# Attention into an activated two-layer product on one core: key blocks in runs of 4, 4, 3, 3, values and first weights in other pieces, and a new order table

## The chip, the cores and the metric

The kernel runs on one core of one Trainium2 chip. A core has TensorE (PE; its weight loads are listed as PEld), VectorE (DVE), ScalarE (ACT), GpSimd (POOL), SyncE (SP, used here to issue transfers) and 16 DMA engines, which the queues of SP and GpSimd share. TensorE's results stand in PSUM, everything else on the chip in SBUF. The metric is the device time of one execution in microseconds.

## The reference

```python
def _attn_ref(q, k, v):                       # 8 x 12 x 448 x 64, float32
    scores = matmul(q, k.T) / sqrt(64) - log(448)
    return matmul(1 / (1 + exp(-scores)), v)
# x: the 12 heads side by side: 3584 tokens x 768
h = x @ w_in                                  # 768 x 2048
g = h * (1 / (1 + exp(-beta * h)))            # beta: one number per hidden column
return g @ w_out                              # 2048 x 768, float32 out
```

The weight is a sigmoid, not a softmax, so no row sum is needed.

## The kernel before

**Layout.** A batch has 448 tokens, cut into 14 blocks of 32. A "group" g is four heads of one batch, three groups per batch and 24 in all; each is loaded as q and k with 32 partitions per head (`load_one`), cast to 16 bits by the transfer. VectorE turns q (`transpose(g, 0)`, step R{g}.0) and k (R{g}.1) with 32x32 transposes, so that the 64 values of a head stand on 32 partitions, in pairs. Keys are used in three full tiles of 128 and a last one of 64 (`JF` = 3, `KL` = 64). Which key of a batch stands in which row of a tile is free as long as k and v agree: before, row group i (32 rows) of the three full tiles holds blocks 3i, 3i+1, 3i+2, and the last tile holds blocks 12 and 13. So v is loaded with four transfers of three blocks and two of one block (`move_v`), and k is turned in two pieces of 384 and 64 words. `double_v_last` (step E) copies the last tile's v to the other 64 partitions.

**Stages.** "Visits" V{g}.{jt} make scores for key tile jt of the four heads (TensorE), then weights by a sigmoid (ScalarE, 128x896). A{g} multiplies the weights with v and VectorE casts the result to xT. In batch 0 the groups 0 to 2 are done in halves of the queries instead (h for scores, y and z for the two parts of the product with v). Then the first dense layer: for all but the first parts of batch 0 with Strassen-Winograd products, steps I{b}.{d}.{p} for P1 to P7, column block d; weight sums S1 to S4 are made once (steps S{i}.{part}, VectorE), token sums are steps X. For batch 0, the first eight column blocks of 128 (dc 0 to 3 and 8 to 11) are done as direct products instead: `dense1`, step f{dc} for the first 224 tokens and D0.{dc} for the other 224. Sigmoid and product with the hidden value follow: on ScalarE and VectorE for the direct blocks, P2 and P3, and on ScalarE and GpSimd in G and B. The second layer is direct for the first two token tiles (O{t}.{half}.{part}) and Winograd after that (U{t}.{p}.{part}, token sums H, weight sums T). Stores go out on SP's queue.

**Order.** Every instruction stands in the order of a table written out by hand or by a planner outside of the kernel: `OPENING`, then `STEPS`. `follow` walks it, and each engine gets its own instructions of the steps in that order. A step such as `w3` puts the transfer of a part of w_in on GpSimd's queue at that place, `v0` the values of batch 0, `Q3` q and k of group 3, `o1.0` a quarter of w_out, `K1` the values of batch 1. `i4` runs four idle units: matmuls on zeros of 512 columns each. GpSimd issues each of its transfers only when the transfer eight places earlier on its queue has landed, since eight semaphores go round. `RAW_HOMES` and `OUT_HOMES` give the buffer for each load and each output in turn. PSUM holds score tiles of two banks each (three at first, two after step p0) and single banks; `bank()` takes the one used longest ago.

**Columns.** Where the next attention step is A or y, `dense` runs each matmul as two halves of 64 output partitions.

**First data.** The first half of q and all of k of group 0 come in 32 bits on SP's queue into the still unused `gt`, are cast by VectorE and ScalarE (`key_cast`) and turned in pieces (`key_turn`). Beta is third on SP's queue.

Of the kernel before, what the change touches and what calls it, by code (L numbers as in the profile page):

```python
# [13 lines left out]
def kernel(  # L14
# [10 lines left out]
    nc = tc.nc  # L25
# [124 lines left out]
    def move_v(queue, to, b: int, h0: int, h1: int):  # L150
        rows = v[b, h0:h1].rearrange("h (p c) d -> p h (c d)", c=NB)
        for i in range(HQ):
            queue.dma_start(
                out=to[i * BLK : (i + 1) * BLK, h0:h1, 0:JF].rearrange("p h j d -> p h (j d)"),
                in_=rows[:, :, JF * i * D : JF * (i + 1) * D],
            )
        rows = v[b, h0:h1].rearrange("h (p c) d -> p h c d", c=NB)
        for c in range(NF, NB):
            lo = (c - NF) * BLK
            queue.dma_start(out=to[lo : lo + BLK, h0:h1, JF], in_=rows[:, :, c])  # L160

    def load_v(b: int, h0: int = 0):
        vs[b] = vp.tile([P, H, JF + 1, D], FP16, tag="v16", name="v16")
        move_v(nc.gpsimd, vs[b], b, h0, H)

    def double_v_last(b: int, h0: int = 0):
        nc.vector.tensor_copy(out=vs[b][KL:P, h0:, JF], in_=vs[b][0:KL, h0:, JF])  # L167

    WCH = 8
    WOUT = 2  # L170

    def load_w_in(c: int):
        n = DFF // WCH
        nc.gpsimd.dma_start(  # L174
            out=w_in16[:, :, c * n : (c + 1) * n],
            in_=moe_w_in[:, c * n : (c + 1) * n].rearrange("(c p) f -> p c f", p=P),
        )
# [34 lines left out]
    def transpose(g: int, r: int, c0: int = 0, c1: int = NB):  # L212
        raw = raws[g][:, r]
        if r == 0:
# [9 lines left out]
        frm = raw.rearrange("p c d -> p (c d)").bitcast(FP32).rearrange("p (c f) -> p c f", c=NB)  # L224
        nc.vector.transpose(
            out=to[:, 0 : JF * P].rearrange("p (j i q) -> p i j q", j=JF, i=HQ),
            in_=frm[:, 0:NF].rearrange("p (i j) f -> p i j f", j=JF),
        )
        nc.vector.transpose(
            out=to[:, JF * P :], in_=frm[:, NF:].rearrange("p c f -> p (c f)")  # L230
        )
# [231 lines left out]
    def wino1(b: int, d: int, p: str):  # L463
# [26 lines left out]
        if p == "P1":  # L490
            nc.scalar.copy(out=osbs[b, d, "a"][:, 0], in_=m)
# [132 lines left out]
    IN_HALVES = 22  # L624

    def store(t: int, lo: int, hi: int):
        osb = osbs[t]
        c, end = t * P, (t + 1) * P
        while c < end:
# [8 lines left out]
            cut = (lo + hi) // 2 if t == IN_HALVES else hi  # L638
# [12 lines left out]
    def share_anew():  # L651
# [9 lines left out]
        "f": lambda dc: dense1(0, dc, 0, QH),  # L661
        "r": lambda g, half: transpose(g, 0, half * NH, (half + 1) * NH),
# [4 lines left out]
        "v": load_v,  # L667
# [27 lines left out]
    def follow(steps):  # L695
# [15 lines left out]
        I0.2.4 E1 I0.3.5 B0.2.0 A3 G0.2 V4.0 I0.3.3 I0.3.7 o1.1 Q7 R5.1 G0.3 O0.0.0 O1.0.0  # L711
        R5.0 V4.2 O0.0.1 Q8 B0.2.1 O0.0.2 I0.3.4 O1.0.1 O1.0.2 V4.3 O1.0.3 B0.3.0 A4 V5.1
        O1.0.4 O1.0.5 O0.0.3 O1.0.6 S1.0 O0.0.4 S3.0 B0.3.1 O1.1.0 R6.1 V5.2 O0.1.0 O0.0.5
        O0.0.6 O1.1.1 R6.0 O0.1.1 S2.0 V5.0 O0.1.2 S4.0 O1.1.2 O1.0.7 O0.1.3 O0.0.7 O1.1.3
        V6.2 O0.1.4 O1.1.4 K2 X1.0 T3.0 T2.0 A5 V6.1 O1.1.5 O1.1.6 R7.0 O1.1.7 O0.1.5 O0.1.6
        I1.3.1 X1.1 R7.1 R8.0 X1.2 V6.0 I1.3.6 I1.3.5 I1.3.2 Q9 R8.1 O0.1.7 V6.3 E2 I1.3.3
        A6 V7.1 T3.1 I1.2.1 I1.3.7 X1.3 G1.3 I1.2.6 I1.2.5 Q11 V7.0 I1.3.4 T2.1 I1.2.2
        B1.3.1 I1.0.1 I1.2.3 B1.3.0 I1.2.7 G1.2 V7.2 I1.0.6 I1.0.5 I1.2.4 R9.0 I1.0.7 I1.0.2
        B1.2.0 B1.2.1 I1.0.3 I1.1.1 G1.0 I1.0.4 B1.0.0 I1.1.6 B1.0.1 Q10 I1.1.5 I1.1.2
        I1.1.7 I1.1.3 V8.0 I1.1.4 B1.1.0 T1.1 A7 B1.1.1 V8.1 R9.1 U2.1.0 U2.1.1 H2.0 H2.1  # L720
        I2.0.1 T4.0 Q12 V8.2 U2.2.0 T1.0 U2.2.1 U2.6.0 K3 H2.2 U2.6.1 H2.3 V8.3 G1.1 T4.1
        U2.5.0 X2.0 U2.5.1 A8 V9.1 K4 U2.3.0 H4.0 U2.3.1 H4.1 U4.1.0 R11.0 U2.7.0 V9.2
        U4.1.1 R11.1 U2.7.1 U4.6.0 U4.6.1 Q13 V9.0 E3 U2.4.0 U2.4.1 H4.2 R10.0 H4.3 R10.1
        U4.5.0 U4.2.0 U4.5.1 U4.2.1 X2.1 X2.3 U4.7.0 U4.7.1 U4.3.0 X2.2 V10.0 U4.3.1 I2.0.6
        U4.4.0 U4.4.1 A9 V10.3 I2.0.5 R12.1 I2.0.2 I2.1.1 I2.1.6 I2.0.3 V10.1 I2.1.2 I2.0.7
        I2.1.5 G2.0 I2.1.7 I2.0.4 I2.1.3 V10.2 I2.1.4 Q15 G2.1 R13.1 I2.2.1 B2.0.0 I2.2.6
        A10 B2.1.0 B2.0.1 V11.0 I2.2.2 B2.1.1 I2.2.5 R13.0 I2.2.7 I2.3.1 I2.2.3 V11.1 I2.2.4
        B2.2.0 I2.3.6 B2.2.1 I2.3.5 G2.2 I2.3.2 I2.3.7 U6.1.0 I2.3.3 V11.2 I2.3.4 R12.0 X3.0
        U6.1.1 B2.3.1 A11 B2.3.0 V12.2 X3.1 H6.0 U6.2.0 H6.1 Q14 U6.2.1 X3.3 I3.0.1 V12.0
        H6.2 I3.0.6 E4 X3.2 G2.3 I3.0.5 U6.6.0 R15.1 U6.6.1 H6.3 V12.1 U6.5.0 U6.5.1 I3.0.2  # L730
        I3.0.7 V12.3 I3.0.3 U6.3.0 R14.0 I3.0.4 U6.7.0 U6.7.1 U6.3.1 A12 B3.0.1 R15.0 B3.0.0
# [12 lines left out]
        I4.3.7 I4.3.3 V17.1 I4.3.4 U12.2.1 U12.5.0 G4.3 B4.3.0 X5.0 U12.5.1 A17 X5.1 V18.1
        B4.3.1 X5.3 I5.0.1 Q23 U12.3.0 U12.7.0 I5.0.6 V18.0 H14.0 U12.7.1 U12.3.1 I5.0.2
# [39 lines left out]
    with tc.manual_schedule():  # L785
# [42 lines left out]
        def key_cast(copy, j: int):  # L828
            copy(out=whole[1][:, :, j], in_=whole[0][:, :, j])
# [50 lines left out]
```

## Time and profile before

| what | value |
|---|---|
| time, median of 3 runs | 367.81 us (366.64 to 368.26) |
| the profiled execution: time / span | 367.32 us / 365.6 us |
| instructions on PE, DVE, ACT, POOL | 3819, 528, 414, 204 |
| moved by DMA | 34.79 MB in 42892 packets, mean 95 GB/s |
| granted TensorE clock | 1.00 |

The span is from the first to the last instruction; the time has 1.7 us around it. Rows of the chain that ended last give start, length, and what the time was spent on. Rows in order of time give start, length, engine, line, operation, out<-in, shape and count; in brackets stands how long the engine was idle before and what ended that. Rows of windows give the busy time (and count) of PE, PEld, DVE, ACT and POOL, then the granted clock, the DMA engines' share, and GB/s. DMA shares above 1 mean that packets overlap.

### The profile page before, as it was taken

What the parts mean: (1) busy time and instruction counts of PE and PEld (TensorE: products, weight loads), DVE (VectorE), ACT (ScalarE), POOL (GpSimd) and SP (SyncE); (2) the same over time, 40 slices, a digit from 0 to 9 for tenths busy, and PEclk for the clock granted to TensorE, in tenths of its full rate; (3) what the DMA queues carried; (4) which work ended last, traced back from release to release, by engine and by line L of the source; (5) the groups of instructions that cost most, each with busy time, mean ns of one, the idle gap of its engine ahead of it and who ended that gap; (6) DMA issues with size and microseconds to landing.
All of it is one profiled execution on the core that took longest, in us unless ns stands there. A gap on an engine that the chain in (4) does not pass through costs nothing.

```text
span 365.6 us, 9439 instructions
## 1 busy us (share of the span) xinstructions
PE 358.9 (98%) x3819; PEld 241.0 (66%) x3819; DVE 279.6 (76%) x528; ACT 250.5 (69%) x414; POOL 168.9 (46%) x204
## 2 busy tenths in 40 slices
PE   7989999999999999999999999999999999999996
PEld 2568654587456785676766676657855688878564
DVE  5439969999977789776787876778768568888755
ACT  5988897799744898775778768766895776537110
POOL 6834486158840376323785444152541026528400
PEclk9999999999999999999999999999999999999999
DMA  8999999930995213153977810694001210110235
GB/s 165 168 198 201 195 204 206 209 61 10 159 180 131 31 23 52 34 105 68 105 123 98 145 45 2 138 127 90 0 4 29 60 45 2 43 29 19 48 81 174
DMA packets 42892, 34.79 MB, mean 95 GB/s; under 512 B 21968, under 2 KB 39520, under 8 KB 42848
## 3 DMA queue, kind: packets, MB, share of 16 engines
q0 software_dynamic: 36688, 22.47, 44.8%
q1 hardware_dynamic: 6160, 11.71, 12.6%
q8 instruction: 30, 0.49, 0.6%
q14 instruction: 14, 0.11, 0.1%
HBM read 45.62 MB, written 11.01 MB: 155 GB/s over the span
## 4 chain that ended last, share of the span: by engine, by line
PE 88%; DMA 6%; POOL 3%; DVE 1%; issue 1%; ACT 0%; POOLq 0%; DVEq 0%; ACTq 0%
PE m_ps L192 70%; PE sco L239 10%; PE av_ps L321 8%; DMA raw<-in_q_dram 3%; DMA raw<-in_k_dram 2%; POOL gt L540 2%; DMA v<-in_v_dram 1%; POOL raw L133 0%; DVE sum L406 0%; POOL gt L530 0%; DVE qT L217 0%; ACT osb L459 0%; DVE v L167 0%; POOL w_in L174 0%; ACT sg L459 0%
## 5 line engine op out<-in xcount | busy, mean ns | idle before, releaser
L251 ACT ACTIVATE attnT<-sco 128x896 f16<-128x896 f32 (+1 forms) x163 | 139.0, 908 | 41.0 <-PE sco L239 40.3
L406 DVE TENSOR_TENSOR osb<-m_ps,osb 128x448 f32<-128x448 f32 (+2 forms) x217 | 127.3, 597 | 49.0 <-PE m_ps L192 35.6
L540 POOL TENSOR_TENSOR gt<-osb,sg 128x448 f16<-128x448 f32 x60 | 68.4, 1157 | 65.3 <-ACT sg L459 65.3
L192 PEld LDWEIGHTS <-w_in 128*128 128x128 f16 (+1 forms) x942 | 76.9, 101 | 14.0 <-issue 7.5
L192 PE MATMUL m_ps<-xT,w_in 128*128 128x224 f16 (+1 forms) x708 | 73.1, 259 | 1.3 <-DMA w_in<-in_moe_w_in_dram 1.2
L530 POOL TENSOR_TENSOR gt<-osb,sg 128x448 f16<-128x448 f32 x30 | 34.5, 1154 | 81.3 <-ACT sg L459 54.1
L459 ACT ACTIVATE sg<-osb,beta_sb 128x448 f32<-128x448 f32 (+1 forms) x120 | 62.5, 576 | 9.3 <-DVE osb L406 8.5
L192 PEld LDWEIGHTS <-sum 128*128 128x128 f16 (+1 forms) x488 | 40.3, 101 | 26.9 <-issue 4.6
L192 PEld LDWEIGHTS <-w_S 128*128 128x128 f16 (+1 forms) x630 | 51.0, 101 | 9.4 <-issue 5.5
L192 PEld LDWEIGHTS <-gt 128*128 128x128 f16 (+1 forms) x434 | 36.2, 100 | 26.3 <-issue 8.5
L192 PE MATMUL m_ps<-w_out,gt 128*128 128x384 f16 (+2 forms) x314 | 53.1, 323 | 0.0
L239 PE MATMUL sco<-qT,kT 32*128 32x448 f16 (+3 forms) x864 | 51.6, 339 | 0.8 <-DVE kT L832 0.5
L192 PE MATMUL m_ps<-xs,w_S 128*128 128x224 f16 (+1 forms) x408 | 42.3, 259 | 0.0
L192 PE MATMUL m_ps<-w_out,sum 128*128 128x384 f16 (+1 forms) x256 | 41.2, 327 | 0.0
L192 PE MATMUL m_ps<-w_T,sum 128*128 128x384 f16 (+1 forms) x232 | 40.4, 326 | 0.2 <-DVE sum L406 0.2
L335 DVE CAST xT<-av_ps 128x448 f16<-128x448 f32 (+1 forms) x54 | 28.2, 564 | 13.2 <-PE av_ps L321 12.9
L321 PE MATMUL av_ps<-attnT,v 128*64 128x448 f16 (+3 forms) x400 | 38.2, 343 | 0.0
L459 ACT ACTIVATE osb<-m_ps,beta_sb 128x224 f32<-128x224 f32 x56 | 22.1, 450 | 16.0 <-PE m_ps L192 10.5
L321 PEld LDWEIGHTS <-v 128*64 128x64 f16 (+1 forms) x432 | 21.2, 108 | 16.8 <-issue 9.5
L239 PEld LDWEIGHTS <-kT 32*128 32x128 f16 (+1 forms) x864 | 13.5, 96 | 22.5 <-issue 19.5
L192 PE MATMUL m_ps<-xT,w_S 128*128 128x224 f16 (+1 forms) x222 | 22.3, 260 | 0.0
L192 PE MATMUL m_ps<-xs,w_in 128*128 128x224 f16 (+1 forms) x234 | 22.1, 260 | 0.0
(55 smaller groups left out, 285.9 us busy)
## 6 DMA issues: line engine op xcount, KB each, us to landing
out_dram<-osb SPq DMA_DIRECT2D x96, 96.0 KB, 1.9
raw<-in_k_dram POOLq DMA_DIRECT2D x23, 224.0 KB, 5.2
raw<-in_q_dram POOLq DMA_DIRECT2D x21, 224.0 KB, 3.7
v<-in_v_dram POOLq DMA_DIRECT2D x32, 144.0 KB, 5.9
w_in<-in_moe_w_in_dram POOLq DMA_DIRECT2D x8, 384.0 KB, 11.3
w_out<-in_moe_w_out_dram POOLq DMA_DIRECT2D x4, 768.0 KB, 11.9
v<-in_v_dram POOLq DMA_DIRECT2D x16, 48.0 KB, 6.0
out_dram<-osb SPq DMA_DIRECT2D x4, 192.0 KB, 1.9
```

The lines of the kernel that those rows point to most:

```text
L192: nc.tensor.matmul(to[c : c + step], hidden[:, c : c + step], weights, **({} if step == P else {"tile_position": (0, c)}), **flags,)
L239: nc.tensor.matmul(sco[base : base + nk, hh, u0 : u0 + n], kT[g][lo : lo + BLK, jt * P : jt * P + nk, e], qT[g][lo : lo + BLK, c0 : c0 + n ...
L251: nc.scalar.activation(out=at[:, :, 0:n], in_=sco[:, :, 0:n], func=AF.Sigmoid, bias=NEG_LOG_S, scale=MSCALE,)
L321: nc.tensor.matmul(av[hh * D : (hh + 1) * D, 0:n], vs[b][base : base + nk, 2 * (s % NPAIR) + hh, jt], at[base : base + nk, hh, 0:n], start ...
L335: nc.vector.tensor_copy(out=xTs[b][:, s % NPAIR, c0 : c0 + n], in_=av[:, 0:n])
L406: nc.vector.tensor_tensor(out=out, in0=in0, in1=in1, op=op)
L459: nc.scalar.activation(out=out, in_=in_, func=AF.Sigmoid, bias=0.0, scale=beta_sb[:, dc : dc + 1])
L530: nc.gpsimd.tensor_tensor(out=gt[:, 2 * d : 2 * d + 2, off : off + QH], in0=ob[:, 0], in1=sg, op=ALU.mult)
L540: nc.gpsimd.tensor_tensor(out=gt[:, dc, off : off + S].rearrange("p (h n) -> p h n", h=2), in0=oa[:, :, j], in1=sg, op=ALU.mult,)
```

## The change

- Keys: the row groups hold runs of 4, 4, 3 and 3 blocks (blocks 0 to 3, 4 to 7, 8 to 10, 11 to 13). v comes with four transfers per batch, in rows of 1024 and 768 bytes as read, instead of six; k is turned in pieces of 256 and 192 words.
- The values of batch 0 come in two parts, four heads (v0.0) and eight heads (v0.1), of four transfers each, and E for them in two steps (e0.0, e0.1).
- w_in comes in five parts instead of eight: two eighths (w0, w1), then three quarters (w2, w3, w4).
- Beta is the first transfer on GpSimd's queue, not the third on SP's; the memset of `dummy` goes from GpSimd to VectorE. In the opening k of group 1 is issued ahead of the first half of its q.
- Blocks 10, 9, 0 and 2 of batch 0 are done at full width (step F: 448 tokens), not as f and D0.
- P1 of batch 0 is copied out of PSUM by VectorE instead of ScalarE.
- Output tile 25 is stored in two halves, as tile 22 was.
- The table and both lists of buffers are new. OPENING and STEPS have 13 idle units instead of 19; ahead of them stand 8 and one of 384 columns instead of 9 and one of 256.

```diff
-        rows = v[b, h0:h1].rearrange("h (p c) d -> p h (c d)", c=NB)
-        for i in range(HQ):
-            queue.dma_start(
-                out=to[i * BLK : (i + 1) * BLK, h0:h1, 0:JF].rearrange("p h j d -> p h (j d)"),
-                in_=rows[:, :, JF * i * D : JF * (i + 1) * D],
-            )
-        for c in range(NF, NB):
-            lo = (c - NF) * BLK
-            queue.dma_start(out=to[lo : lo + BLK, h0:h1, JF], in_=rows[:, :, c])
+    RUNS = ((0, JF + 1), (JF + 1, JF + 1), (2 * JF + 2, JF), (3 * JF + 2, JF))
+    GROUP0 = (0, HQ), (HQ, H)
+        rows = v[b, h0:h1].rearrange("h (p c) d -> p h (c d)", c=NB)
+        for i, (c, n) in enumerate(RUNS):
+            nc.gpsimd.dma_start(
+                out=vs[b][i * BLK : (i + 1) * BLK, h0:h1, 0:n].rearrange("p h j d -> p h (j d)"),
+                in_=rows[:, :, c * D : (c + n) * D],
+            )
...
+    def turn_keys(to, raw, i: int, j0: int, j1: int):
+        to = to.rearrange("p (a b) -> p a b", b=2 * BLK)[:, i::2]
+        n = JF + 1 - i
+        c = 2 * i * (JF + 1) * D // PAIR
+        frm = raw[:, c : c + 2 * n * D // PAIR].rearrange("p (i j q) -> p i j q", i=2, j=n)
+        nc.vector.transpose(
+            out=to[:, j0:j1].rearrange("p j (i q) -> p i j q", i=2), in_=frm[:, :, j0:j1]
+        )
...
-    WCH = 8
+    W_IN = (0, DFF // 8, DFF // 4, DFF // 2, 3 * DFF // 4, DFF)
...
-            nc.scalar.copy(out=osbs[b, d, "a"][:, 0], in_=m)
+            copy = nc.scalar.copy if b else nc.vector.tensor_copy
+            copy(out=osbs[b, d, "a"][:, 0], in_=m)
...
-    IN_HALVES = 22
+    IN_HALVES = (22, 25)
...
+        "F": lambda dc: dense1(0, dc),
...
-        idle_units(9)
-        idle_units(1, 256)
+        idle_units(8)
+        idle_units(1, 384)
```

The new order up to I0.2.3, the step on which the prediction's sum hangs:

```diff
     OPENING
+        k1 h0.0.0 l1.0.0 h0.0.1 i1 R1.1 k2 r1.0 i1 i1 i1 i1 l1.0.1 h1.0.0 l2.0.0 l0.0.1 i1
+        R2.1 i1 v0.0 r0.1 r2.0 h1.0.1 i1 i1 e0.0 r1.1 i1 i1 v0.1 h2.0.0 y0.0 w0 z0.0 h2.0.1
+        y1.0 e0.1 w1 z1.0 h1.1.0 b0 w2 y2.0 z2.0 l2.0.1 h0.1.0 i1 f1 h0.1.1 w3 i1 p0 Q3 f3
+        r2.1 y0.1 h1.1.1 z0.1 I0.3.1 I0.2.1 h2.1.0 y1.1 z1.1 X0.0 w4 I0.2.2 I0.3.2 h2.1.1
     STEPS
+        R3.0 f8 f11 y2.1 Q4 z2.1 R3.1 K1 X0.1 o0.0 Q5 X0.3 o1.0 F10 D0.1 D0.8 o0.1 D0.11
+        S1.1 V3.2 S3.1 R4.0 F9 o1.1 D0.3 V3.1 S2.1 R4.1 Q6 F0 F2 X0.2 V3.0 I0.2.6 I0.2.5
+        V3.3 S4.1 I0.2.7 I0.3.6 V4.1 I0.2.3 E1 I0.2.4 A3 V4.0 I0.3.5
...
```

The old order of the same stretch:

```diff
     OPENING
-        l1.0.0 h0.0.0 k1 b0 l2.0.0 i4 r1.0 k2 R1.1 h0.0.1 v0 R2.1 l0.0.1 i4 l1.0.1 h1.0.1 i4
-        w0 w1 w2 r2.0 h1.0.0 i2 i2 h2.0.1 E0 w3 i3 h2.0.0 r0.1 y0.0 z0.0 h0.1.0 r1.1 y1.0
-        l2.0.1 z1.0 h0.1.1 y2.0 z2.0 w4 p0 h1.1.0 Q3 w5 f1 f0 f3 r2.1 I0.2.1 h1.1.1 y0.1
-        z0.1 I0.3.1 h2.1.0 y1.1
     STEPS
-        R3.0 z1.1 I0.3.2 I0.2.2 w6 h2.1.1 w7 Q4 X0.0 f9 f2 y2.1 z2.1 X0.1 X0.3 f8 D0.10 D0.9
-        R3.1 o0.0 K1 D0.1 D0.0 D0.2 Q5 S1.1 S2.1 V3.1 D0.11 D0.8 D0.3 S3.1 V3.2 I0.2.6
-        I0.2.5 o1.0 V3.3 X0.2 f11 R4.1 R4.0 o0.1 V3.0 S4.1 I0.2.7 Q6 f10 I0.3.6 V4.1 I0.2.3
-        I0.2.4 E1 I0.3.5 B0.2.0 A3 G0.2 V4.0 I0.3.3 I0.3.7 o1.1 Q7 R5.1
...
```

More of the change, by code (lines that the diff above doesn't have):

```diff
@@ L223, in transpose @@
         to = kT[g].rearrange("p k e -> p (k e)").bitcast(FP32)
[L224 to L227, printed above, removed]
-        )
-        nc.vector.transpose(
-            out=to[:, JF * P :], in_=frm[:, NF:].rearrange("p c f -> p (c f)")
-        )
+        frm = raw.rearrange("p c d -> p (c d)").bitcast(FP32)
+        for i in range(2):
+            turn_keys(to, frm, i, 0, JF + 1 - i)
     def score_tile():
@@ L714 @@
[L714 to L731, printed above, removed]
@@ L805 @@
         nc.vector.memset(still, 0.0)
-        beta_in = sigp.tile([P, S], FP32, tag="sg", name="beta_in")[0:BLK, 0:P]
-        nc.vector.memset(beta_in, 0.0)
         def idle_units(n: int, cols: int = 512):
```

192 lines of the change are left out of this document (99 added, 93 removed).

## The prediction

> **What bounds the kernel now.** I read the page first, then the waits of TensorE, then the chain that ended last, then the opening in order of time.
>
> ```profile
> span 365.6 us, 9439 instructions
> PE 358.9 (98%) x3819; PEld 241.0 (66%) x3819; DVE 279.6 (76%) x528; ACT 250.5 (69%) x414; POOL 168.9 (46%) x204
> DMA  8999999930995213153977810694001210110235
> ```
>
> TensorE is busy for 98% of the span, and the DMA engines are full only for the first eight slices (73 us). So this is a TensorE-bound kernel with a DMA-fed opening.
>
> ```profile
> PE idle_ps L812 <- DVE gt L805: 1.2, 1, 1.2
> PE m_ps L192 <- DMA w_in<-in_moe_w_in_dram: 1.2, 2, 0.9
> ...
> PE m_ps L192 <- DVE sum L406: 0.2, 1, 0.2
> PE m_ps L192 <- DVE xT L335: 0.2, 1, 0.2
> ```
>
> These are the waits of TensorE but two (us in total, times, longest); the two left out are short ones on key turns in the first 10 us. Of the four, 2.8 us, only the 0.2 us on `sum` lies behind the opening. The rest of what can be won is the idle units, matmuls on zeros that fill a known wait. The chain that ended last shows the place from which nothing but matmuls follows:
>
> ```profile
> 28.84 1.34 PE m_ps L192 x24
> ...
> 43.35 1.85 PE m_ps L192 x36
> ...
> 308.51 53.94 PE m_ps L192 x408
> 362.47 0.36 DVE osb L406
> ```
>
> The x24 at 28.84 are f9 and f2. The x36 at 43.35 are the steps I0.2.3, I0.2.4 and I0.3.5, in column halves. From 43.35 to 362.45 there are 319.1 us of matmuls, then 3.1 us for the last add and store.
>
> **The sum hangs on one step.** I compared the two tables. In both, I0.2.3 comes after the same products: all eight direct blocks, P1, P2, P5, P6, P7 of column block 2 and P1, P2, P6 of block 3, the twelve half visits, V3.0 to V3.3 and V4.1. What comes after it is the same set too, so the 319.1 us are the same. Changed time = 367.32 us (this execution; 0.49 below the median of 367.81) + (start of I0.2.3 − 43.35) + new waits behind it. The start of I0.2.3 is the later of two arrivals: TensorE, and VectorE with the weight sum S4.1, which I0.2.3 reads.
>
> **TensorE's arrival.** The last place where a transfer sets TensorE's pace ahead of I0.2.3 is y1.1 (attention of group 1, second query half):
>
> ```profile
> 24.61 0.75 PE L192 MATMUL m_ps<-xT,w_in 128*128 128x224 f16 x6 [0.92 <-DMA w_in<-in_moe_w_in_dram]
> 24.79 0.41 DVE L217 STREAM_TRANSPOSE qT<-raw 128x224 f32<-128x224 f32 x1 [2.27 <-DMA raw<-in_q_dram]
> 25.10 0.55 POOL L133 DMA_DIRECT2D raw<-in_q_dram  x1 [2.66 <-DMA w_in<-in_moe_w_in_dram]
> 25.12 0.65 DVE L335 CAST xT<-av_ps 128x224 f16<-128x224 f32 x2
> 25.80 0.98 PE L321 MATMUL av_ps<-attnT,v 128*64 128x224 f16 x16
> 31.03 3.63 PE L192 MATMUL m_ps<-xT,w_in 128*128 128x224 f16 x36
> ```
>
> VectorE waits 2.27 us for the second half of q of group 2 (step r2.1), then casts two attention outputs, and only then are two banks free for y1.1 at 25.80. The changed queue holds the same bytes ahead of that transfer: k and q of groups 0 to 2, all of v, half of w_in (two eighths and a quarter for four eighths), plus 8 KB of beta. What changes is the length of the rows:
>
> ```profile
> 8.40:11.50 3.10, 2.86 (x40) 1.17 (x39) 1.64 (x5) 2.41 (x5) 2.11 (x4) 1.00 1.58 186
> 11.20:17.20 6.00, 5.93 (x97) 3.05 (x95) 2.18 (x6) 5.83 (x8) 5.68 (x8) 1.00 1.39 168
> 17.20:24.50 7.30, 6.24 (x104) 4.27 (x96) 2.34 (x7) 6.54 (x11) 2.48 (x3) 1.00 1.35 184
> 29.00:34.70 5.70, 5.70 (x80) 5.11 (x80) 5.59 (x16) 4.14 (x9) 1.84 (x3) 1.00 1.40 201
> 46.90:54.80 7.90, 7.90 (x92) 4.77 (x85) 4.64 (x10) 7.46 (x13) 7.67 (x10) 1.00 1.30 206
> ```
>
> The last column is GB/s moved, in bytes as written. Values in rows of 768 bytes (first window, mostly) ran at 186, eighths of w_in in rows of 1024 bytes (fourth) at 201, w_out in rows of 1536 bytes (fifth) at 206. v writes 0.69 MB per batch: 3.7 us at 186, 3.5 at a mean of 195, so 0.2 us. A quarter of w_in writes 0.79 MB: 3.9 us at 201, 3.8 at 206, so 0.1 us (nothing to 0.3). I take 0.3 us for both: r2.1 at 24.5, y1.1 at 25.5.
>
> From y1.1 to I0.2.3 the kernel before needs 43.35 − 25.80 = 17.55 us. The changed table has in that stretch 14 half blocks of direct products where the old one has 13 (f0 was made earlier). The x36 at 31.03 are six of them, 0.6 us each: +0.6. The 0.2 us wait on xT goes: −0.2.
>
> Four blocks (F10, F9, F0, F2) take 24 matmuls of 448 columns for 48 of 224, with four products and sigmoids for eight. No row has a 448-column matmul on the full array. The 3.63 us for 36, less a 0.26 us tail, make 96 ns for 224 columns, so two cost 193 ns. Bounds for one of 448: 193 (nothing won) and 187 (columns at the 2.4 per ns that TensorE has at a granted clock of 1.00, if one fixed part of 3 ns goes twice). I take −0.1 us, between 0 and −0.15. The Trainium skill, "TensorE: Matmul & The Clock Gate", section "Back-to-back issue gap", gives N / 2.4 + 2.5 ns at full clock; by it the 24 would save 0.06 us.
>
> P1 of batch 0 is now copied by VectorE, not ScalarE. Price, by the nearest row:
>
> ```profile
> L391 DVE COPY osb<-m_ps 128x384 f32<-128x384 f32 x4 | 2.2, 538 | 0.4 <-PE m_ps L192 0.3
> ```
>
> So 0.55 to 0.62 us each (538 × 448/384 at most). Both copies now stand on VectorE behind r2.1 and the two casts: 24.5 + 0.4 + 0.6 + 1.1 = 26.6. P2 adds into the same bank, so I0.2.2 waits for its copy, while TensorE gets there at 25.5 + 0.9 = 26.4. Cost 0.2, at most 0.5, nothing if r2.1 is earlier than I think. Cover gone, the price is VectorE's backlog; ScalarE had room.
>
> Sum: 25.5 + 17.55 + 0.6 − 0.2 − 0.1 + 0.2 = **43.55**.
>
> **VectorE's arrival.** The last part of w_in releases S1.1, and everything in the queue behind it:
>
> ```profile
> 33.08 0.61 POOL L153 DMA_DIRECT2D v<-in_v_dram  x1 [1.39 <-DMA w_in<-in_moe_w_in_dram]
> 35.12 0.61 POOL L160 DMA_DIRECT2D v<-in_v_dram  x1 [1.42 <-DMA w_in<-in_moe_w_in_dram]
> 35.49 0.95 DVE L406 TENSOR_TENSOR w_S<-w_in 128x1536 f16<-128x1536 f16 x1
> ...
> 39.15 1.35 DVE L406 TENSOR_TENSOR osb<-m_ps,osb 128x448 f32<-128x448 f32 x2
> 40.41 0.50 DVE L406 TENSOR_TENSOR xT<-xT 128x672 f16<-128x672 f16 x1
> 40.83 0.38 DVE L363 TENSOR_TENSOR gt<-m_ps,sg 128x224 f16<-128x224 f32 x1
> 41.13 0.57 DVE L225 STREAM_TRANSPOSE kT<-raw 128x384 f32<-128x384 f32 x1
> 41.75 0.60 DVE L217 STREAM_TRANSPOSE qT<-raw 128x448 f32<-128x448 f32 x1
> 42.27 0.92 DVE L406 TENSOR_TENSOR w_S<-w_in,w_S 128x1536 f16<-128x1536 f16 x1
> 43.11 0.61 DVE L406 TENSOR_TENSOR osb<-m_ps,osb 128x448 f32<-128x448 f32 x1
> ```
>
> GpSimd issues a transfer only when the one eight places ahead has landed; the first two rows show the last eighths of w_in landing 2.0 us apart, the last just ahead of 35.12 (TensorE saw the fourth at 24.61, GpSimd at 25.10, so 34.6 to 35.1). With larger rows the changed kernel has w4, its last part, by 34.5. TensorE reads w3 in f8, at 25.5 + 28.84 − 25.80 = 28.5; r2.1's transfer and a quarter behind it make 28.4, so there is no wait and no margin. S1.1 stands behind the product of D0.11: F10 starts where f8 did, at 25.5 + 31.03 − 25.80 = 30.7, F10 and three half blocks are 3.0 us, a sigmoid and a product 0.8 more: 34.5, the same moment. From the start of S1.1 to the end of S4.1 VectorE has, by the rows above (where work follows at once, from start to start): four weight sums (0.95 each), R4.0 (0.52), R4.1 (0.62; two transposes of 256 and 192 words for two of 384 and 64), three products of 448 columns (0.61 each, as the add) and one of 224 (0.30), a token sum (0.42), two adds (1.26). That is 8.8 us: S4.1 ends at 43.3, 0.2 us ahead of TensorE. w4 may be 0.2 us late for nothing; after that each us costs a us.
>
> **What is hidden or cancels.** The table has 13 idle units for 19, and 8.75 for 9.5 ahead of it. They are fillers: where y1.1 is set by a transfer, fewer of them leave a wait, not time. Beta ahead of k on GpSimd's queue takes the place of that queue's memset and puts half of q behind k; k of group 1 is still second. First scores need two key turns, not one (+0.25 us at 5.5), hidden by the same transfer. Later values take four issues for six, 1.2 us of GpSimd per batch, where GpSimd is 46% busy. A second store in halves (tile 25) lies ahead of the last store.
>
> So the forecast is 43.55 − 43.35 = +0.2: **367.5 us**, with 0.1 for a new short wait, **367.6**.
>
> **Rivals.**
> (1) *The opening's queue runs at its later rate.* From 11.2 to 24.5 it wrote 168 × 6.0 + 184 × 7.3 = 2.35 MB. If its dip comes from the many short rows and goes, 201 GB/s bring r2.1 1.6 us earlier. Then the sigmoids that y1.1 reads are the bound:
>
> ```profile
> 22.88 1.35 ACT L251 ACTIVATE attnT<-sco 128x896 f16<-128x896 f32 x2 [0.18 <-PE sco L239]
> ```
>
> They end at 24.2, so y1.1 moves from 25.5 to 24.2, the copies of P1 are done in time (−0.2), w4 comes earlier with the rest: I0.2.3 at 42.05, 366.0. For it: the dip is there. Against: the transfers from 17.2 to 24.5 are like those from 29.0, and slower.
> (2) *Slower: eight pieces of v starve the queue.* v of batch 0 now goes in eight small pieces, each issued when the one eight places ahead has landed:
>
> ```profile
> 3.61 2.58 POOL L153 DMA_DIRECT2D v<-in_v_dram  x4
> 11.11 3.30 POOL L174 DMA_DIRECT2D w_in<-in_moe_w_in_dram  x4 [0.21 <-issue]
> ```
>
> The last piece must wait for the last half of q, near 11.5, so w_in is first issued near 12.4 to 13.2, not 11.11. It decides when less is queued at 11 us than the engines move until then; every us of drought moves r2.1, w3, w4 and I0.2.3 by one. At 1.3 to 2.1 us: 368.9 to 369.7, middle 369.3. The Trainium skill speaks for this one: "DMA: Bandwidth & Descriptors", section "Bandwidth", asks for transfers of 1 MiB and calls those under 64 KB bound by descriptors; pieces of 98 to 262 KB lie between. Against: four issues in 2.58 us here kept the queue full.
> (3) *A new wait behind I0.2.3.* The last quarter of w_out now goes ahead of q of group 6. From w4 to that transfer stand 5.0 MB (all of w_out 3.15, v 0.69, q and k of groups 4 and 5 0.92, the transfer 0.23), 24.4 us at 204 GB/s: 58.9. Step R6.0 comes 15.3 us of matmuls behind I0.2.3, at 58.9 as well. So a queue that is late by more than rival 1's gain makes VectorE wait there with TensorE's bank copies behind it: 1 us or so, 368.6.
>
> **How the numbers follow.** Forecast 0.45 (366.9 to 368.3), rival 1 0.25, rival 2 0.2, rival 3 0.1. A measurement of this kernel tells about 0.5% (1.84 us around 367.81) from no change: faster means below 365.97, slower above 369.65. Below lies a good half of rival 1: 0.15. Above lie the upper half of rival 2 and sums of 2 and 3 with the unknown prices: 0.23. Same: 0.62. The range goes from 365.7 (rival 1 with 0.3 more from the unknown prices) to 370.0 (the top of rival 2 with 0.3 more).
>
> **What would show it.** r2.1 near 24.5, y1.1 near 25.5, I0.2.2 waiting for a VectorE copy; I0.2.3 (the first 12 half-column matmuls on w_S and xT behind V4.1) near 43.5, with S4.1 done before it; 319.1 us of matmuls behind it. It would be wrong if r2.1 moves by over 1 us, if S1.1 starts after 35.3, or if TensorE's waits behind 45 us add up to over 1 us.

## The result, and the profile after

The changed kernel takes 368.55 us (median of 19 runs, 367.19 to 371.05), the kernel before 366.84 us beside it (19 runs): a ratio of 1.0048, 95% interval 1.0031 to 1.0064. So it is slower by 1.71 us in the medians; the forecast was 367.6 us with no difference that can be told. A second set of runs gave 1.0050 (1.0036 to 1.0064).

The profiled execution of the changed kernel took 368.81 us. From its page, the span, the busy shares, the granted clock and the DMA share of the 40 slices:

```profile
span 367.0 us, 9218 instructions
PE 359.8 (98%) x3720; PEld 237.6 (65%) x3720; DVE 282.3 (77%) x528; ACT 247.5 (67%) x408; POOL 159.6 (43%) x189
PEclk9999999999999999999999999999999999999999
DMA  8999999963389150511896149803000300301037
```

TensorE is as busy as before, with 99 matmuls fewer. The waits of TensorE (us in total, times, longest):

```profile
PE idle_ps L815 <- DVE gt L810: 1.3, 1, 1.3
PE sco L247 <- ACT early L259: 0.8, 1, 0.8
PE sco L247 <- DVE kT L178: 0.8, 1, 0.8
PE m_ps L205 <- DVE osb L414: 0.3, 1, 0.3
PE m_ps L205 <- DVE gt L371: 0.3, 1, 0.3
```

The wait on w_in is gone from this list (a second profile of the changed kernel, below, has it back), and two waits of 0.8 us on the first scores have come, both ahead of 8 us. The fourth is new as well; it lies at 77.6 us. The chain that ended last, at the three places of the sum, and VectorE and TensorE around y1.1 in order of time:

```profile
44.27 1.27 PE m_ps L205 x24
...
302.20 61.29 PE m_ps L205 x468
363.51 0.36 DVE osb L414
```
```profile
25.40 0.41 DVE L230 STREAM_TRANSPOSE qT<-raw 128x224 f32<-128x224 f32 x1 [0.91 <-DMA raw<-in_q_dram]
25.73 0.65 DVE L343 CAST xT<-av_ps 128x224 f16<-128x224 f32 x2
26.71 0.99 PE L329 MATMUL av_ps<-attnT,v 128*64 128x224 f16 x16
```

r2.1 is at 25.40 for a forecast of 24.5, y1.1 at 26.71 for 25.5, I0.2.3 at 44.27 for 43.55. From I0.2.3 to the last matmul, 363.49, are 319.2 us (319.1 before), and the span ends 3.5 us after that (3.1 before). Against the first profile the 1.5 us of span are thus 0.92 + 0.1 + 0.4 to 0.5.

**The first profile of the kernel before was not a typical one.** A second profile of the same kernel, taken among the experiments (time and ratio in the table below), has a span of 364.7 us. Its rows for the same places (r2.1, y1.1, the start of I0.2.3, the last matmuls):

```profile
23.76 0.41 DVE L217 STREAM_TRANSPOSE qT<-raw 128x224 f32<-128x224 f32 x1 [1.24 <-DMA raw<-in_q_dram]
...
24.74 0.99 PE L321 MATMUL av_ps<-attnT,v 128*64 128x224 f16 x16
```
```profile
42.47 1.85 PE m_ps L192 x36
...
307.64 53.94 PE m_ps L192 x408
```

r2.1 is 1.03 us earlier than in the first profile and everything behind it by 0.9. So the forecast was built on an execution whose opening queue happened to be a microsecond late. A second profile of the changed kernel (span 366.6) has these rows in its chain, and these among the waits of TensorE, both in the opening:

```profile
44.02 1.27 PE m_ps L205 x24
...
301.70 61.29 PE m_ps L205 x468
```
```profile
PE av_ps L329 <- DMA v<-in_v_dram: 1.3, 1, 1.3
...
PE m_ps L205 <- DMA w_in<-in_moe_w_in_dram: 0.9, 1, 0.9
```

Second profile against second profile: I0.2.3 at 44.02 for 42.47, +1.55; behind it 301.70 + 61.29 − 44.02 = 318.97 for 319.11, −0.14; end of the span 3.6 for 3.2 us behind the last matmul, +0.4. The sum, 1.85 us, is the difference of the spans, and near the 1.71 us of the medians.

### The profile page after: what moved, and what is told of

It is laid out like the page before. It is cut to its first block, busy times and chain, and to the rows that moved or that the text cites. A ratio compares the mean times of both kernels' runs of the same rounds, so it can differ in the third digit from the quotient of the medians.

```text
span 367.0 us, 9218 instructions
## 1 busy us (share of the span) xinstructions
PE 359.8 (98%) x3720; PEld 237.6 (65%) x3720; DVE 282.3 (77%) x528; ACT 247.5 (67%) x408; POOL 159.6 (43%) x189
## 3 DMA queue, kind: packets, MB, share of 16 engines
q1 hardware_dynamic: 6272, 11.71, 12.4%
## 4 chain that ended last, share of the span: by engine, by line
PE 86%; DMA 6%; DVE 3%; POOL 2%; ACT 1%; SPq 1%; issue 1%; ACTq 0%; DVEq 0%
PE m_ps L205 69%; PE sco L247 9%; PE av_ps L329 8%; DMA raw<-in_q_dram 3%; DMA out_dram<-osb 2%; DMA raw<-in_k_dram 2%; POOL v L160 1%; POOL w_in L187 1%; ACT attnT L259 1%; SPq L649 1%; DVE xT L343 0%; DVE osb L399 0%; DVE osb L500 0%; POOL raw L133 0%; DVE osb L414 0%
## 5 line engine op out<-in xcount | busy, mean ns | idle before, releaser
L205 PEld LDWEIGHTS <-w_in 128*128 128x128 f16 (+1 forms) x924 | 74.6, 101 | 15.5 <-issue 9.0
L205 PE MATMUL m_ps<-xT,w_in 128*128 128x224 f16 (+2 forms) x684 | 73.2, 263 | 0.6 <-DVE osb L414 0.3
L247 PE MATMUL sco<-qT,kT 32*128 32x448 f16 (+3 forms) x864 | 52.6, 347 | 1.6 <-ACT early L259 0.8
L160 POOL DMA_DIRECT2D v<-in_v_dram x36 | 22.0, 618 | 10.1 <-DMA w_in<-in_moe_w_in_dram 6.2
```

The lines of the kernel that those rows point to most:

```text
L160: nc.gpsimd.dma_start(out=vs[b][i * BLK : (i + 1) * BLK, h0:h1, 0:n].rearrange("p h j d -> p h (j d)"), in_=rows[:, :, c * D : (c + n) * D],)
L205: nc.tensor.matmul(to[c : c + step], hidden[:, c : c + step], weights, **({} if step == P else {"tile_position": (0, c)}), **flags,)
L247: nc.tensor.matmul(sco[base : base + nk, hh, u0 : u0 + n], kT[g][lo : lo + BLK, jt * P : jt * P + nk, e], qT[g][lo : lo + BLK, c0 : c0 + n ...
```

## The experiments

All profiles in one table. "First w_in" is when GpSimd issues w0, "r2.1's data" when the transfer lands on which r2.1 waits; behind and tail are counted from I0.2.3 to the last matmul and from there to the end of the span. The ratio is to the kernel before on the same chip. Each row of times is one execution, and the ratio comes from 5 to 19 runs.

| kernel | first w_in | r2.1's data | y1.1 | I0.2.3 | behind | tail | ratio, 95% interval |
|---|---|---|---|---|---|---|---|
| before, 1st profile | 11.11 | 24.76 | 25.80 | 43.35 | 319.1 | 3.1 | |
| before, 2nd (c_before) | 10.54 | 23.73 | 24.74 | 42.47 | 319.1 | 3.2 | 0.9996, 0.9984 to 1.0008 |
| after, 1st | 11.41 | 25.37 | 26.71 | 44.27 | 319.2 | 3.5 | 1.0048, 1.0031 to 1.0064 |
| after, 2nd (c_after) | 11.32 | 25.22 | 26.46 | 44.02 | 319.0 | 3.6 | 1.0050, 1.0036 to 1.0064 |
| e1, v in four | 9.00 | 23.65 | 26.51 | 44.06 | 318.6 | 3.6 | 1.0034, 1.0017 to 1.0051 |
| e2, idle units | 11.43 | 25.00 | 26.25 | 43.81 | 320.1 | 3.5 | 1.0075, 1.0058 to 1.0091 |
| e3, both | 8.85 | 22.43 | 25.49 | 43.04 | 319.7 | 3.5 | 1.0065, 1.0044 to 1.0086 |
| e4, tile 25 whole | 11.39 | 25.14 | 26.39 | 43.94 | 319.3 | 3.5 | 1.0073, 1.0048 to 1.0097 |
| e5, K3 later | 11.37 | 24.75 | 25.98 | 43.54 | 318.7 | 3.6 | 1.0042, 1.0029 to 1.0055 |
| e6, end of table | 11.79 | 26.02 | 27.25 | 44.82 | 320.0 | 3.4 | 1.0069, 1.0053 to 1.0085 |
| e7, old table | 8.33 | 23.81 | 24.80 | 42.42 | 319.5 | 3.2 | 1.0011, 1.0001 to 1.0020 |
| e8, and w_in in five | 8.31 | 22.98 | 25.87 | 43.47 | 319.1 | 3.2 | 1.0039, 1.0027 to 1.0051 |
| e9, e1 + e4 + e5 + e6 | 9.10 | 23.82 | 26.01 | 43.56 | 318.8 | 3.4 | 1.0031, 1.0018 to 1.0045 |
| e10, e9 + e2 | 8.99 | 23.52 | 25.48 | 43.03 | 318.8 | 3.4 | 1.0018, 1.0004 to 1.0032 |
| e11, e7 + eight pieces | 11.94 | 26.90 | 27.90 | 45.51 | 319.1 | 3.2 | 1.0057, 1.0040 to 1.0075 |
| e12, old opening, new rest | 8.62 | 23.99 | 24.99 | 42.64 | 319.0 | 3.4 | 1.0007, 0.9992 to 1.0022 |

Four theories. **S**: eight small pieces of v starve the opening's queue. **C**: TensorE's clock stays low at the start and holds up scores and sigmoids. **B**: a buffer makes TensorE wait at 77 us. **Q**: the last stores are too many. The rival to S and C together was that the larger parts of w_in come too late.

**e1 to e3: the queue and the clock.**

```diff
-        "v": lambda b, part: load_v(b, *GROUP0[part]),
+        "v": lambda b, part: load_v(b) if part == 0 else None,
```

> The changed kernel with the values of batch 0 in one part of four transfers (all twelve heads, at the place of v0.0) instead of two parts of four. Theory S (the eight small pieces slow the opening's queue): the queue moves about as much between 9 and 17 us as before the change, w0 lands near 17.2 instead of 17.97, r2.1 near 24.7 instead of 25.40, I0.2.3 near 43.5 instead of 44.27, and the time is 0.7 to 0.9 us below the changed kernel's. Theory C (the clock of TensorE stays low until some 13 us, and the chain of scores and sigmoids behind it arrives no earlier): the transfers land earlier, but I0.2.3 and the time move by less than 0.3 us. Theory T (neither: the larger parts of w_in are what is late): w0 not earlier, time within 0.2 us.

e2 changes the idle units, e3 makes both edits:

```diff
-        idle_units(8)
+        idle_units(10)
...
-        k1 h0.0.0 l1.0.0 h0.0.1 i1 R1.1 k2 r1.0 i1 i1 i1 i1 l1.0.1
+        k1 h0.0.0 l1.0.0 i4 h0.0.1 i1 R1.1 k2 r1.0 i1 i1 l1.0.1
```

> The changed kernel with more idle units where TensorE has nothing to do (ten for eight ahead of the table, four more behind the first scores, two fewer later). Theory C: TensorE's idle units run at 0.21 us each from an earlier time, scores of group 1 come up to 0.5 us earlier, ScalarE's waits of 1.75 us shrink, and if that chain is what is late at y1.1, the time falls by 0.5 to 0.9 us. Theory S: w2 and the second half of q of group 2 land where they did (24.8 and 25.4), so y1.1 stays near 26.7 and the time within 0.2 us of the changed kernel's.

> Both of the edits before this one together: values of batch 0 in four transfers, and more idle units early. If queue and cold clock each arrive late by about the same (S and C together), only this one gains: 0.7 to 0.9 us below the changed kernel's, r2.1 near 24.7. If S alone is right it gives what the first of the three gives; if C alone is right, what the second gives.

In e1 the data of r2.1 come 1.7 us earlier, more than S asked for, and y1.1 moves by 0.2 only: TensorE itself gets there no sooner. This profile took 368.18 us, though, and the median of e1's eleven runs is 367.31. By the medians e1 is 0.9 us behind the kernel before, where the changed kernel is 1.7; by the ratios, 1.0034 for 1.0048, it gains 0.5 us, and their intervals overlap. So S may be worth more in most executions than in the profiled one. In e2 TensorE starts y0.0 2.3 us earlier (13.27 for 15.55) and then waits 1.1 us for w_in at 24.48: y1.1 gains 0.5. With both, y1.1 gains 1.2 and I0.2.3 as well. So in the profiles S and C are both true, and each hides the other, as the third expectation had it for that case. Yet the times of e2 and e3 are no better than the changed kernel's, and the gain of 0.5 to 0.9 us that all three expectations named did not come in either of them. What they win ahead of I0.2.3 they lose behind it, 320.1 and 319.7 us for 319.2; e1, without such a loss, has 318.6. That is where theory B came from.

**e4 and e6: the end.**

```diff
-    IN_HALVES = (22, 25)
+    IN_HALVES = (22,)
```

> The changed kernel with output tile 25 stored whole again (only tile 22 in halves). Theory Q (the queue of SP issues the last stores back to back and the extra issues push the last one behind VectorE's last add): SP's issues end within 0.1 us of the last add, the tail from the last matmul to the end of the span is 3.1 to 3.2 us instead of 3.5, the time 0.2 to 0.4 us less. Rival (the extra issues are hidden, the tail is set by the transfer itself): tail 3.4 to 3.5, time the same within 0.1 us.

e6 leaves tile 25 in halves and moves two steps:

```diff
-        U26.6.1 U26.5.1 U22.4.1 U26.2.1 H26.3 U26.7.0 U20.4.1 U26.3.0 U26.7.1 U24.4.1 U26.3.1
+        U26.6.1 U26.5.1 U20.4.1 U22.4.1 U26.2.1 H26.3 U26.7.0 U24.4.1 U26.3.0 U26.7.1 U26.3.1
```

> The changed kernel with two steps at the end of the table moved forward: the last parts of P4 for tiles 20 and 24 (U20.4.1 ahead of U22.4.1, U24.4.1 ahead of U26.3.0), so that the stores of tiles 21 and 25 are issued earlier, as in the kernel before; the products are the same. Theory Q2 (at the end, stores land one by one, about 0.5 us apart, and too many of them are left behind the last matmul; a store less alone did not help): the tail from the last matmul to the end of the span goes from 3.5 to between 3.1 and 3.3 us. Rival (the tail is set by the last store alone, whatever is ahead of it): 3.5 us, as before.

SP's issues in the last stretch, in the changed kernel and in the second profile of the kernel before:

```profile
354.36 10.24 SPq L649 DMA_DIRECT2D out_dram<-osb  x18
```
```profile
352.53 9.87 SPq L640 DMA_DIRECT2D out_dram<-osb  x13
```

The new end has 18 stores where the old one has 13. One less (e4) brought the last issue to the last add, but the tail only from 3.55 to 3.53 us: its expectation failed, since the store then waited behind others that landed 0.5 us apart. Two tiles stored earlier (e6) brought 3.38, for an expected 3.1 to 3.3. Both together (e9, e10) 3.35, for 3.16 with the old end (e7). So Q holds in direction; 0.2 of the 0.4 us stay unexplained.

**e5: the buffer.**

```diff
-        X1.1 O1.1.7 I1.3.1 T2.0 V6.0 I1.3.6 I1.3.5 O0.1.7 K3 T2.1 Q9
+        X1.1 O1.1.7 I1.3.1 T2.0 V6.0 I1.3.6 I1.3.5 O0.1.7 T2.1 Q9
...
-        U2.2.1 H2.1 T4.1
+        U2.2.1 H2.1 K3 T4.1
```

> The changed kernel with step K3 (values of batch 3, four transfers) moved in the table from behind the last part of O0.1 to behind H2.1, some ten us later. Theory B (behind I0.2.3 a buffer makes TensorE wait at 77.6 us: ScalarE's copy of P1 of batch 1 needs a buffer whose store was issued at 70.4 and landed only at 76.3, behind twelve loads): the store lands near 73 to 74, ScalarE's copy is not held up, the wait of 0.3 us on osb at 77.6 is gone, and the matmuls behind I0.2.3 take 318.6 to 318.8 us instead of 319.2, as in the kernel with the values of batch 0 in four transfers, where this wait was missing: time 0.3 to 0.6 us less. Rival (the wait is VectorE's backlog, not the store): the wait on osb stays at 0.3 us, time the same.

The chain of the changed kernel ahead of the wait at 77.6 us:

```profile
68.39 0.36 SPq L649
...
69.25 1.10 SPq L649
...
70.40 5.89 DMA out_dram<-osb
76.39 0.54 ACT osb L500
76.95 0.64 DVE osb L414
77.63 4.91 PE m_ps L205 x48
```

ScalarE may copy P1 of batch 1 only when the output that stands in its buffer is stored; that store took 5.89 us from issue to landing; VectorE adds into the copy, and TensorE waits for the bank. In e5 the loads of batch 3 are out of the way:

```profile
74.97 0.53 ACT L500 COPY osb<-m_ps 128x448 f32<-128x448 f32 x1 [0.25 <-DMA out_dram<-osb]
```
```profile
43.54 1.27 PE m_ps L205 x24
...
300.92 61.29 PE m_ps L205 x468
```

300.92 + 61.29 − 43.54 = 318.67 us, with no wait of TensorE left there. So the wait costs 0.55 us in the first profile of the changed kernel, though its row shows 0.3, and 0.3 in the second. The chain (store, copy, add, matmul) is shown: in nine of the ten profiles with the new table from the start, ScalarE's copy begins 0.10 us after that store has landed.

What makes the store late is not shown. It takes 5.4 to 6.4 us from issue to landing in all ten, 5.81 in e5 against 5.89 in the changed kernel, so moving the loads of batch 3 did not shorten its way. What differs is its issue: 25.5 to 25.6 us behind I0.2.3 in the four profiles without the wait (e1, e5, e9, e10) and 25.8 to 26.7 in the six with it. In those six an issue of SP ahead of it took 0.8 to 1.6 us instead of about 0.5, as the row at 69.25 shows. Moving K3 may be what cured this, since e5, e9 and e10 have it; but e1 has no such wait either, with K3 in its old place. The time of e5, 1.0042, is 0.2 to 0.3 us below the changed kernel's, which is within the noise.

The wait costs 1.0 us in e3 and 1.2 in e6. In e2, 0.8 of the 1.4 us lost belong to it; the other 0.55 are lost before, from 62.3 us on, where TensorE waits 0.16 us for a key turn whose transfer, issued at 41.0, landed at 61.5. That is why e2 and e3 gave back what they won.

**e7, e8, e11: the parts of the change under the old table.**

> The changed code under the old table: key blocks in runs of 4, 4, 3, 3, values in four transfers per batch (no second part), beta first on GpSimd's queue; but w_in in eight parts, P1 copied by ScalarE, eight direct half blocks, old buffers, old idle units, only tile 22 in halves. My prediction's size for the rows of the values was 0.2 us. If it is right, r2.1 lands near 24.6 and the time is within 0.3 us of the kernel before. Theory R (longer rows of values speed up the queue by more than I took: with the values in four transfers and w_in in five parts the same transfer landed 1.1 us earlier than in the kernel before): r2.1 lands at 23.7 to 24.2 and the time is 0.5 to 1 us less than the kernel before. Rival: the first keys in runs of four come later (5.97 instead of 5.50 for the first scores), TensorE's clock stays low for longer, and the time is the same or up to 1 us more.

> As the one before it, with w_in in five parts as well (w2 for w2 and w3, w3 for w4 and w5, w4 for w6 and w7, at the place of the first of each pair). My prediction's size for this was 0.1 us at r2.1. The quarter w2 lands whole and f1 waits for all of it where before it waited for an eighth: no loss at r2.1, which stands behind it. If rows of w_in matter, r2.1 lands 0.1 to 0.3 us earlier than in the run before it; if larger parts hurt, TensorE waits 0.5 to 1 us more on w_in ahead of y1.1, and the time is 0.3 to 0.8 us more.

The edits of e7 to the changed kernel (the two lists of buffers and both tables are the old ones), then that of e8 to e7:

```diff
-        "v": lambda b, part: load_v(b, *GROUP0[part]),
+        "v": load_v,
-    IN_HALVES = (22, 25)
+    IN_HALVES = (22,)
-            copy = nc.scalar.copy if b else nc.vector.tensor_copy
+            copy = nc.scalar.copy
-        idle_units(8)
-        idle_units(1, 384)
+        idle_units(9)
+        idle_units(1, 256)
-    W_IN = (0, DFF // 8, DFF // 4, DFF // 2, 3 * DFF // 4, DFF)
+    W_IN = tuple(i * DFF // 8 for i in range(9))
```
```diff
-    W_IN = tuple(i * DFF // 8 for i in range(9))
+    W_IN = (0, DFF // 8, DFF // 4, DFF // 2, 3 * DFF // 4, DFF)
```

e7's data of r2.1 land at 23.81, within 0.1 us of the second profile of the kernel before, and its ratio is 1.0011: together, the runs of keys, four transfers of v for six, the longer rows of v and beta first bring and cost next to nothing. Theory R, that longer rows speed up the queue, falls. (My expectation had compared with the first profile of the kernel before.) In e8 the data of r2.1 come 0.8 us earlier, but I0.2.1 waits 1.4 us for a whole quarter of w_in, and I0.2.3 is 1.05 us later: larger parts of w_in hurt by 1 us where nothing else is late. That is what became of the 0.1 us that the prediction took off for them. So the rival to S and C is real as well.

e11 is e7 with the pieces back, and nothing else:

```diff
-        "v": load_v,
+        "v": lambda b: [load_v(b, *part) for part in GROUP0],
```

> The changed code under the old table, as in the run with that name, but with the values of batch 0 in two parts of four transfers, one right behind the other, at the place of the old v0. The same bytes in the same order on the queue, only in eight pieces instead of four. Theory S: the pieces slow the queue as they do under the new table, where r2.1 lands at 24.8 to 26.0 with eight pieces and at 22.4 to 23.8 with four: r2.1 goes from 23.8 to between 24.8 and 25.5, I0.2.3 from 42.35 to between 43.3 and 44, and the time goes up by 0.9 to 1.6 us against the run with four. Rival (the new order of the queue is what slows it, beta and k first, not the pieces): r2.1 within 0.3 us of 23.8, the time the same.

Issues on GpSimd's queue and two windows (the last column GB/s), first e7, then e11:

```profile
4.12 2.49 POOL L160 DMA_DIRECT2D v<-in_v_dram  x4
8.33 0.85 POOL L187 DMA_DIRECT2D w_in<-in_moe_w_in_dram  x1
```
```profile
11.00:13.00 2.00, 2.00 (x37) 0.94 (x36) 0.35 (x1) 1.85 (x4) 1.83 (x3) 1.00 1.44 193
13.00:15.00 2.00, 1.94 (x33) 0.85 (x27) 0.41 (x1) 1.85 (x4) 1.34 (x3) 1.00 1.44 204
```
```profile
4.11 2.94 POOL L160 DMA_DIRECT2D v<-in_v_dram  x5
8.40 1.29 POOL L160 DMA_DIRECT2D v<-in_v_dram  x2 [1.34 <-DMA raw<-in_k_dram]
10.28 0.57 POOL L160 DMA_DIRECT2D v<-in_v_dram  x1 [0.59 <-DMA raw<-in_k_dram]
11.94 3.33 POOL L187 DMA_DIRECT2D w_in<-in_moe_w_in_dram  x4
```
```profile
11.00:13.00 2.00, 2.00 (x29) 0.85 (x28) 0.37 (x2) 1.86 (x4) 2.00 (x4) 1.00 1.32 157
13.00:15.00 2.00, 1.94 (x37) 0.80 (x30) 0.41 (x1) 1.85 (x4) 2.00 (x3) 1.00 1.02 140
```

S is shown under the old table, and by more than expected: the same bytes in eight pieces put the first w_in 3.6 us later on the queue, the DMA engines move 157 and 140 GB/s where they moved 193 and 204, r2.1's data land 3.1 us later, and the time goes from a ratio of 1.0011 to 1.0057, some 1.7 us. (The profiled execution of e11, 369.51 us, is the slowest of its seven runs; their median is 368.69.) The rival (the new order of the queue) is out, since e11 has the old one. GpSimd issues only when the transfer eight places ahead has landed, so each small piece takes the place of a large one in the row of eight; the large one is then issued too late to follow without a gap.

The table says the same across all profiles. Where w0 is issued by 9.1 us, r2.1's data land at 22.4 to 24.0; at 10.5, 23.7; at 11.1, 24.8 (the first profile of the kernel before); at 11.3 to 11.4, 24.8 to 25.4; at 11.8 and 11.9, 26.0 and 26.9. The two profiles of the kernel before stand on this slope too: 0.57 us in the issue, 1.03 us in the landing. Below 10.5 us the slope ends: e7 issues w0 2.2 us ahead of the second profile of the kernel before, and the data land at the same time.

**e9, e10, e12: what is left.**

> The changed kernel with three edits at once: values of batch 0 in four transfers, K3 later, and the tail (U20.4.1 and U24.4.1 earlier, tile 25 stored whole). If the three losses are separate, they add: I0.2.3 near 43.0 to 44.0 (the clock of TensorE in the opening decides), no wait at 77 us, 318.7 us behind I0.2.3, tail 3.2 to 3.3 us: 1.3 to 2 us less than the changed kernel, about the time of the kernel before. If the opening is limited by TensorE's low clock in most executions, the gain is 0.8 us and the kernel stays slower than before by 0.8.

> As the one before it, with the more numerous idle units early as well. With queue, clock, buffer and tail all cured: y1.1 near 25.5, I0.2.3 near 43.0, 318.7 us behind it, tail 3.2 us: span near 364.9 us, 2 us less than the changed kernel and 0.3 to 0.8 us less than the first profile of the kernel before. If the extra idle units cost more than they bring (in two kernels they made the median worse than the profile), it is no better than the one before it.

> The changed code under the old table up to I0.2.3 (values in four transfers, w_in in eight) and the new table from there on, with K3 later, the two steps at the end earlier and tile 25 stored whole. It puts together what the runs so far show as good: I0.2.3 near 42.4 as in the second profile of the kernel before, 318.7 us behind it for 319.2, tail 2.4 us from the last matmul to the last landing for 2.2. Sum 0.3 us less than the kernel before, that is 364.4 us of span and a ratio of 0.999. If I0.2.3 stays near 43.0, as in the version with all cures under the new table, the new order ahead of it is not what costs there.

Their edits are those above put together; e12 is e7 with the new lists of buffers (those of the first two Winograd outputs exchanged) and, from I0.2.3 on, the steps of e9, with o1.1 ahead of them. e9 and e10 differ in the idle units alone: 0.53 us at I0.2.3, 0.46 us in the medians (367.57 and 367.11; the intervals of their ratios overlap). That is the price of C once the queue is cured. e10 recovers most of the loss and stays at 1.0018; its I0.2.3 is 0.56 us behind the old kernel's at equal data. e12 with the old opening has 42.64 there. So the rest lies in what e10 and e12 have different ahead of I0.2.3: the order, w_in in five parts, and P1's copies on VectorE; no run separates these. No version beats the kernel before: e12, the best, can't be told from it. The 0.3 us that I expected of it are not there. Its I0.2.3 is 0.2 us later than expected, and its stretch behind is 319.0 and not 318.7, because of A3 at its start:

```profile
43.91 0.10 issue
44.01 1.64 PE av_ps L329 x16
```

The last of the four transfers of batch 1's values lands at 43.88, and A3 starts 0.13 us later; its 16 matmuls take 1.64 us, for 1.45 in the second profile of the kernel before. e7 has the same at 44.27, and 319.5 us behind. With the new runs each of the four transfers brings rows of the first three key tiles, so A3 needs all four; before, it could begin while the two pieces for the last tile were still on their way (44.15, with the last one landing at 44.58).

## Why the prediction was wrong, point by point

- **TensorE's arrival at y1.1, with r2.1 at 24.5: wrong, and this is the step that failed.** The sum said "The changed queue holds the same bytes ahead of that transfer" and took 0.3 us off for longer rows. Bytes were the wrong unit: the number of transfers in the row of eight decided when w_in was issued. The longer rows of v were worth nothing (e7). r2.1 came at 25.40 and 25.25 for 23.76 in the second profile of the kernel before: +1.5 to +1.6 us, not −0.3. The sum also took it that r2.1 alone sets y1.1. In the first profile of the changed kernel the casts behind r2.1 end at 26.38 and y1.1 follows at 26.71, right behind TensorE's own work; in the second TensorE had waited 0.86 us for the quarter w2 until 24.69, and y1.1 is at 26.46. So three delays arrive together there: the transfer, TensorE's slow opening (C), and the larger parts of w_in (1 us in e8), which the sum had as nothing or a gain.
- **Rival 2 was the right story for the queue.** It named the eight pieces and gave 368.9 to 369.7 us; the profiled time is 368.81, the median 368.55. It got 0.2 because "four issues in 2.58 us here kept the queue full", which was read off four pieces, not eight. Its own sum expected w_in at 12.4 to 13.2; it was issued at 11.41, and that was late enough. That the time comes near its range is in part luck: the wait at 77 us and the new end, 0.7 to 1 us together in the two profiles, were not in its sum, and the pieces are not alone in the opening's loss. The page of the Trainium skill that spoke for it ("DMA: Bandwidth & Descriptors", section "Bandwidth") was right in direction: 157 GB/s with the pieces at 11 to 13 us, 193 without. But what the rows of e11 show is late issues, not a price of small transfers as such.
- **The base was one execution.** 43.35 was taken as the kernel's own; a second profile has 42.47. The median of 367.81 came from three runs; over 19 it is 366.84. And with 19 runs of each a difference of 0.16% can be told, not 0.5%: the band of "same" was three times too wide. The dip of the opening's queue, which rival 1 wanted to cure, is smaller there. In the first profile, then in the second:

```profile
13.00:15.00 2.00, 1.94 (x31) 1.03 (x29) 1.04 (x2) 1.86 (x3) 2.00 (x4) 1.00 1.14 149
17.00:19.00 2.00, 1.99 (x48) 1.30 (x48) 0.92 (x3) 2.00 (x3) 0.84 (x1) 1.00 1.11 145
```
```profile
13.00:15.00 2.00, 1.94 (x31) 1.03 (x29) 0.77 (x2) 1.85 (x3) 1.92 (x4) 1.00 1.38 194
17.00:19.00 2.00, 2.00 (x48) 1.29 (x48) 0.91 (x3) 2.00 (x3) 0.83 (x1) 1.00 1.27 169
```

- **From y1.1 to I0.2.3: 17.56 us for a forecast of 18.05.** The one more half block is there, but a stall that the first trace hid inside a row is gone: V3.0's eight matmuls took 0.98 us in the kernel before and 0.57 in the changed one, as the rows below show, the first of the kernel before. The copies of P1 on VectorE made nothing wait (0.2 forecast), while F10 waits 0.26 us for the product that frees its bank, which I had not seen.

```profile
40.01 0.98 PE L239 MATMUL sco<-qT,kT 32*128 32x448 f16 x8
```
```profile
40.16 0.57 PE L247 MATMUL sco<-qT,kT 32*128 32x448 f16 x8
```

- **VectorE's arrival** was right in kind: w4 landed at 35.18, S4.1 ended just ahead of I0.2.3. The bound that I gave for "wrong", S1.1 after 35.3, was passed (35.79).
- **Idle units as "fillers" and the first key turns as "hidden": wrong.** Where more of them fill the pauses, TensorE's clock rises earlier (last section). C costs 0.5 us where the queue is cured (e9, e10) and at most about a quarter of a us where it isn't (the two profiles of the changed kernel, y0.0 at 15.55 and 13.19, I0.2.3 at 44.27 and 44.02).
- **319.1 us behind I0.2.3: right as a number, by two errors.** Without the new wait it is 318.7 (a wait of 0.2 us on `sum` is gone, and fewer matmuls are cut in column halves, 3232 for 3306 behind I0.2.3); the wait at 77 us gives 0.3 to 0.55 back. Rival 3 looked for a new wait behind I0.2.3 at a transfer of q near 59 us; in the changed kernel it was a buffer at 77, and only e2 lost time near rival 3's place, at 62.3.
- **The second store in halves (tile 25) as hidden: wrong.** The new end costs 0.4 to 0.5 us; the halves are the least of it.

By the second profiles, the loss is made up so: some 1.55 us ahead of I0.2.3 (the pieces, with the clock, the larger parts of w_in and the new order of the opening beside them), −0.1 behind it, 0.4 at the end. How much of the 1.55 belongs to each of the four can't be said in one number, since they hide each other.

## What to carry to other kernels

Count transfers, not only bytes, ahead of the one that matters: where a kernel lets only so many be under way on a queue, each small one takes a large one's place, and the price appears several transfers later. Take the base of a sum from two profiles where the stretch is set by a transfer: here one execution was 0.9 us off in exactly the place that the forecast hung on. And when a cure shows nothing, look for the second limit that arrives at the same time, and further on for a wait that takes the gain back, before dropping the theory.

## What was not expected of the hardware

TensorE ran at half rate for much longer in the changed kernel's opening, while the row of the granted clock on the page shows 9 in all slices. An idle unit is a matmul of 512 columns. In the changed kernel, then the second profile of the kernel before, then e10:

```profile
8.94 2.31 PE L815 MATMUL idle_ps<-gt 128*128 128x512 f16 x5
```
```profile
6.21 1.04 PE L812 MATMUL idle_ps<-gt 128*128 128x512 f16 x4
```
```profile
6.79 1.04 PE L813 MATMUL idle_ps<-gt 128*128 128x512 f16 x4
```

Less the tail of about 0.2 us, that is 0.42 us for one at 9 us in the changed kernel, and 0.21 us for one at 6 us in the others. In its first profile the changed kernel's TensorE had been at work since 1.33 us but for two waits of 0.8 us ahead of 8 us. Between its profiles the end of the low rate moved by several us. In e9 the clock's own record shows it, in the window's third column from the right:

```profile
5.00:9.00 4.00, 2.40 (x36) 1.04 (x36) 2.56 (x10) 2.93 (x5) 2.63 (x5) 0.88 1.11 166
9.00:11.00 2.00, 2.00 (x20) 0.66 (x18) 0.98 (x4) 0.56 (x2) 1.90 (x3) 0.50 1.32 181
```

The Trainium skill, "TensorE: Matmul & The Clock Gate", section "Part 1: The HAM clock gate", has a clock of half rate until the unit has been busy for a window of some 3.4 us, a window that runs freely and so falls differently from run to run. The spread from run to run agrees; the length does not, with half rate at 9 to 11 us here in two kernels whose TensorE paused only for 0.7 to 0.9 us at a time. That those pauses are what kept the clock low is suggested by e10, which fills them, but is not shown: the second profile of the changed kernel has pauses of 0.6 and 0.8 us too, and its five idle units at 8.21 us took only 1.25 us.
